# Clustered attention followed by an MLP: heads in pairs in a hand-given order, transposes from SBUF, argmax by block transposes, MLP pieces spread over the next batch

## The chip, the cores and the metric

The kernel runs on one core of a Trainium2 chip. The metric is the device time of one execution in microseconds (us). All runs named here were in the fast state but one, a run of e16 that is left out of its median. A profiled execution's span (582.5 us for the kernel before) is the time that the trace covers; it differs from the median time by under 2%. PE is the matrix engine (TensorE), PEld its weight loads; VectorE is DVE, ScalarE is ACT, GpSimd is POOL, and SyncE (SP) issues most transfers in these kernels. A suffix q (SPq, ACTq) marks an engine's queue of issued transfers and waits. In the timelines below each engine works through its own instructions in the order in which the program gives them. PSUM is the memory into which the matmuls write; a buffer there is free again once another engine has read it out.

## The reference, cut to what matters

```python
# q, k, v: (4 batches, 8 heads, 768 tokens, 64); centroids: (8 heads, 16, 64)
q_assign = argmax(q_n @ c_n.T);  k_assign = argmax(k_n @ c_n.T)      # normalised rows
mask   = q_assign[:, :, :, None] == k_assign[:, :, None, :]
scores = where(mask, q @ k.T / 8, -1e9)
attn   = exp(scores - max);  attn /= sum(attn)
x      = (attn @ v), heads side by side                              # (3072, 512)
h      = x @ w_in                                                    # (3072, 2048)
out    = (h * sigmoid(h)) @ w_out                                    # (3072, 512)
```

Both kernels write each token's cluster as a one-hot of 16 rows below the 64 rows of q and k, so that one matmul over 80 rows gives score and mask. The exp runs on the transposed scores. The row of ones beside v gives the denominators, and the attention output is multiplied by their reciprocals before the MLP (called MoE in the code). The clusters come from "logits": q and k are split into a high and a low f16 part (128 rows), multiplied by the centroids' high part and, for accuracy, by their low part.

## The kernel before

One head at a time goes through stages that a software pipeline spaces out. The order within an engine is chosen by the framework. The parts that matter:

```python
wout_s = ...; nc.gpsimd.dma_start(wout_s, moe_w_out...)       # 2 MB of f16 in one transfer, w_in likewise
nc.vector.tensor_scalar(out=wout_s, in0=wout_s, scalar1=0.5, ...)     # L59
... # stage_p2, p3: hl -> DRAM scratch, then dma_start_transpose(ab, DRAM)
def stage_l(bh):                                              # logits of one head, q and k
    for ti, ab in enumerate((qab, kab)):
        g = ti * 32
        for half in range(2):
            nc.tensor.matmul(dst, stk[:, h],   ab[:, sl],    start=True, stop=False)   # 128 rows
            nc.tensor.matmul(dst, clT32[:, h], ab[0:64, sl], start=False, stop=True)   # 64 rows
    nc.scalar.copy(Lsb[:, 0], psL...); nc.scalar.copy(Lsb[:, 1], psL...)
    nc.gpsimd.partition_all_reduce(mx, Lsb, channels=16, reduce_op=max)     # L176
# stage_l2: oh_sb = Lsb >= mx (VectorE); stage_m: one-hots into ab[64:80]
# stage_b1: scores and exp (L199); stage_b2: P @ v; stage_z1, z2: denominators out,
#           reciprocal, back as one row, partition_broadcast on GpSimd, multiply on VectorE
# MoE of a 384-token block: 16 pieces A (h, tanh, product), then 3 pieces B (output)
```

The softmax here doesn't subtract the row's maximum and nothing guards it: scores larger than these inputs give would overflow.

## Time and profile before

| | before |
|---|---|
| median time | 579.92 us (first three runs), 579.76 us (four) |
| first exp, last exp (start) | 72.3 us, 478.9 us |
| PE busy | 437.3 us, 75% of the span |
| mean granted clock | 0.899 |

The page's first part (busy time, share of the span, instructions):

```profile
PE 437.3 (75%) x1922; PEld 201.6 (35%) x1922; DVE 326.3 (56%) x498; ACT 301.2 (52%) x419; POOL 217.0 (37%) x104
```

The page's fourth part, the chain of waits that ended last, by engine:

```profile
PE 36%; ACT 15%; DVE 14%; POOL 14%; DMA 11%; issue 8%; SPq 2%; DVEq 0%; POOLq 0%; ACTq 0%
```

Busy time by stretch: start, attention, and what is left after the last exp. In each row come the stretch, its length, and busy us with the number of instructions for PE, PEld, DVE, ACT and POOL; then the granted clock, the DMA engines' busy share and GB/s.

```profile
0.00:72.00 72.00, 15.89 (x38) 3.96 (x39) 27.84 (x66) 8.87 (x11) 28.07 (x20) 1.00 0.95 174
72.00:480.00 408.00, 335.46 (x1468) 157.24 (x1468) 256.66 (x361) 259.32 (x353) 185.76 (x82) 0.86 0.44 89
480.00:583.00 103.00, 86.01 (x417) 40.37 (x415) 41.83 (x72) 33.05 (x57) 3.14 (x3) 0.99 0.09 32
```

The reader should see that no engine is full: PE is on the chain for 36% of the time only, and the clock in the middle is 0.86, so part of PE's "busy" time is matmuls at half speed (384-column matmuls stand 0.16 us apart in dense stretches and 0.32 us after a gap of 2.84 us, at 214 us).

Two details: the first is VectorE's wait at the start, a timeline line (start, duration, instruction, and in brackets the idle time before it and what ended it). The second is the pace of the logit matmuls: the timeline's first column shows them 0.27 us apart for 384 columns, taking turns between 128 and 64 rows.

```profile
27.46 2.29 DVE L59 TENSOR_SCALAR wout_s<-wout_s 128x8192 f16<-128x8192 f16 x1 [21.21 <-DMA wout_s<-in_moe_w_out_dram]
...
219.42 0.33 PE L171 MATMUL psL<-ab_1456,clT_89 64*32 64x384 f16 x1
219.68 0.34 PE L170 MATMUL psL<-ab_1456,stk 128*32 128x384 f16 x1
219.95 0.33 PE L171 MATMUL psL<-ab_1456,clT_89 64*32 64x384 f16 x1
```

### The profile page before, as it was taken

How to read it: one execution, taken by the hardware profiler on the slowest of the kernel's cores; microseconds unless marked ns; L12 is line 12 of the kernel's file. 1: busy time of each engine (PE TensorE's matmuls, PEld its weight loads, DVE VectorE, ACT ScalarE, POOL GpSimd, SP SyncE). 2: the span in 40 equal slices, each digit the busy share in tenths (PEclk: the TensorE clock that was granted, in tenths of full speed). 3: DMA queues.
4: the chain of work that ended last, by engine and by line, in shares of the span. 5: the costliest groups of instructions: out<-in, count | busy, mean ns of one | idle time of the engine just before them, and what ended most of it. 6: DMA issues, size and time to landing. Idle time of an engine off the chain costs nothing.

```text
span 582.5 us, 5887 instructions
## 1 busy us (share of the span) xinstructions
PE 437.3 (75%) x1922; PEld 201.6 (35%) x1922; DVE 326.3 (56%) x498; ACT 301.2 (52%) x419; POOL 217.0 (37%) x104
## 2 busy tenths in 40 slices
PE   0005489757688578998578798789898999897976
PEld 0001134323233233444234344334444454343433
DVE  2162699975848966687855535442455335425251
ACT  1002377648368575747476447664487393415150
POOL 1053854655466544444474235444433002000000
PEclk9999998769679678799798898779798999999999
DMA  8999566957455544857552212323120100100101
GB/s 155 190 150 245 125 182 156 152 116 117 76 110 117 87 119 102 161 137 222 98 108 35 36 54 37 48 33 60 46 30 1 41 17 20 38 37 19 52 2 55
DMA packets 106190, 52.20 MB, mean 90 GB/s; under 512 B 84080, under 2 KB 102512, under 8 KB 106160
## 3 DMA queue, kind: packets, MB, share of 16 engines
q1 hardware_dynamic: 78480, 44.49, 30.8%
q0 software_dynamic: 27680, 7.34, 13.2%
q8 instruction: 15, 0.25, 0.2%
q14 instruction: 15, 0.12, 0.1%
HBM read 27.49 MB, written 19.07 MB: 80 GB/s over the span
## 4 chain that ended last, share of the span: by engine, by line
PE 36%; ACT 15%; DVE 14%; POOL 14%; DMA 11%; issue 8%; SPq 2%; DVEq 0%; POOLq 0%; ACTq 0%
POOL mx L176 13%; PE po L265 10%; PE ph L254 9%; ACT P L199 6%; DMA wout_s<-in_moe_w_out_dram 4%; ACT tn L259 4%; DVE gt L260 4%; PE pO L209 4%; PE psL L170 4%; PE psL L171 3%; PE pST L196 3%; DVE oh_sb L182 3%; ACT Lsb L174 2%; PE pO L210 2%; DMA rzd<-rzt 1%
## 5 line engine op out<-in xcount | busy, mean ns | idle before, releaser
L199 ACT ACTIVATE P<-pST,bias_77 128x768 f16<-128x768 f32 x192 | 161.5, 909 | 65.3 <-PE pST L197 64.1
L176 POOL PARTITION_ALL_REDUCE mx<-Lsb x32 | 153.7, 4807 | 109.8 <-ACT Lsb L174 109.7
L259 ACT ACTIVATE tn<-ph,zbias 128x384 f32<-128x384 f32 x128 | 73.0, 588 | 105.1 <-PE ph L254 104.2
L260 DVE SCALAR_TENSOR_TENSOR gt<-tn,ph 128x384 f16<-128x384 f32 x128 | 68.7, 551 | 80.9 <-ACT tn L259 80.1
L182 DVE TENSOR_TENSOR oh_sb<-Lsb,mx 16x1536 f16<-16x1536 f32 x32 | 66.8, 2087 | 66.5 <-POOL mx L176 66.5
L265 PE MATMUL po<-wout_s,gt 128*128 128x512 f16 x384 | 87.2, 383 | 2.7 <-DVE gt L260 2.7
L254 PEld LDWEIGHTS <-win_s 128*128 128x128 f16 x512 | 51.9, 101 | 96.7 <-issue 69.2
L209 PE MATMUL pO<-P,vt 128*65 128x512 f16 x192 | 84.1, 457 | 0.5 <-ACT osb L212 0.5
L254 PE MATMUL ph<-xt_73,win_s 128*128 128x384 f16 x128 | 44.2, 346 | 48.2 <-DVE gt L260 35.6
L173 ACT COPY Lsb<-psL 16x768 f32<-16x768 f32 x32 | 25.2, 788 | 93.9 <-PE psL L171 86.3
L142 POOL DMA_DIRECT2D vt<-in_v_dram x32 | 27.9, 878 | 88.1 <-DVE vt L141 54.5
L210 PE MATMUL pO<-P,vt 128*65 128x256 f16 x192 | 59.8, 311 | 0.0
L233 POOL PARTITION_BROADCAST rzb<-rzrow x32 | 34.6, 1082 | 66.8 <-DMA rzrow<-rzd 66.6
L265 PEld LDWEIGHTS <-gt 128*128 128x128 f16 x384 | 37.8, 99 | 47.9 <-issue 5.6
L254 PE MATMUL ph<-xt_74,win_s 128*128 128x384 f16 x128 | 44.4, 348 | 5.6 <-DVE xt_74 L234 5.6
L254 PE MATMUL ph<-xt_76,win_s 128*128 128x384 f16 x128 | 43.8, 342 | 5.5 <-DVE xt_76 L234 5.5
L254 PE MATMUL ph<-xt_75,win_s 128*128 128x384 f16 x128 | 44.0, 346 | 1.1 <-DVE xt_75 L234 1.1
L270 DVE COPY ot<-po 128x512 f32<-128x512 f32 x24 | 16.4, 687 | 41.4 <-PE po L265 41.2
L209 PEld LDWEIGHTS <-vt 128*65 128x65 f16 x192 | 25.4, 132 | 38.1 <-issue 27.3
L170 PEld LDWEIGHTS <-stk 128*32 128x32 f16 x128 | 12.2, 95 | 67.1 <-issue 64.5
L210 PEld LDWEIGHTS <-vt 128*65 128x65 f16 x192 | 24.9, 130 | 8.5 <-issue 1.5
L212 ACT COPY osb<-pO 65x768 f32<-65x768 f32 x32 | 25.6, 801 | 0.2 <-PE pO L210 0.2
(493 smaller groups left out, 508.4 us busy)
## 6 DMA issues: line engine op xcount, KB each, us to landing
out_dram<-ot SPq DMA_DIRECT2D x24, 256.0 KB
vt<-in_v_dram POOLq DMA_DIRECT2D x32, 96.0 KB, 3.9
win_s<-in_moe_w_in_dram POOLq DMA_DIRECT2D x1, 2048.0 KB, 13.6
wout_s<-in_moe_w_out_dram POOLq DMA_DIRECT2D x1, 2048.0 KB, 25.3
zd<-osb SPq DMA_DIRECT2D x32, 3.0 KB
zt<-zd SPq DMA_DIRECT2D x32, 3.0 KB
rzd<-rzt SPq DMA_DIRECT2D x32, 3.0 KB
rzrow<-rzd SPq DMA_DIRECT2D x32, 3.0 KB
```

The costliest lines, as they stand in the source:

```text
L142: nc.gpsimd.dma_start(vt[:, :, 0:64], v[b, h].rearrange("(j p) d -> p j d", j=NJ))
L170: nc.tensor.matmul(dst, stk[:, h], ab[:, sl], start=True, stop=False)
L176: nc.gpsimd.partition_all_reduce(mx, Lsb, channels=HC, reduce_op=bass_isa.ReduceOp.max)
L182: nc.vector.tensor_tensor(out=oh_sb, in0=Lsb, in1=mx, op=ALU.is_ge)
L199: nc.scalar.activation(out=P, in_=pST[:, 0:768], func=AF.Exp, bias=bias32, scale=ESC)
L209: nc.tensor.matmul(pO[:, 0:512], vt[:, j, :], P[:, 0:512], start=(j == 0), stop=(j == NJ - 1))
L210: nc.tensor.matmul(pO[:, 512:768], vt[:, j, :], P[:, 512:768], start=(j == 0), stop=(j == NJ - 1))
L233: nc.gpsimd.partition_broadcast(rzb, rzrow, channels=64)
L254: nc.tensor.matmul(ph, win_s[:, r, ts(fb, 128)], xts[r][:, T0 : T0 + MOE_T], start=(r == 0), stop=(r == NR - 1),)
L259: nc.scalar.activation(out=tn, in_=ph, func=AF.Tanh, bias=zbias, scale=0.5)
L260: nc.vector.scalar_tensor_tensor(out=gt[:, fb, :], in0=tn, scalar=1.0, in1=ph, op0=ALU.add, op1=ALU.mult)
L265: nc.tensor.matmul(po, gt[:, fc, ts(tsub, 128)], wout_s[:, fc, :], start=(fc == 0), stop=(fc == NFB - 1),)
```

## The change

The intent is to keep PE fed throughout. Two heads (a pair) are routed together. The clusters are found with VectorE's 32x32 block transposes, instead of ScalarE copies and GpSimd's maximum. The scratch in DRAM goes: transposes read SBUF. Denominators come back as a broadcast transfer to 64 partitions. Weights come in eight pieces. The 0.5 moves to the output copy. Every instruction stands in an order written by hand: the program is cut into slots, each with one score tile (six to a head, twelve to a pair), and each batch's MoE is cut into 56 pieces, spread over the slots of the next batch. The core of the diff:

```diff
-    for i in range(nbh + OF_P0 - OF_Z2):        # stages of one head, order by the framework
-        if valid(i): stage_p0(i)
-        ...
+    ctx.enter_context(tc.manual_schedule())
+    def logits(p):                              # a pair: 2 heads x (q, k) = 4 column groups
+        for u, (lo, hi) in enumerate(((0, 512), (512, 768))):
+            for i, w in enumerate((wh, wl)):    # both 128 rows
+                for h in range(2):
+                    for t in range(2):
+                        g = 32 * (2 * h + t)
+                        nc.tensor.matmul(psL[g : g + 32, 0 : hi - lo], w[:, 2 * r + h], ab[:, h, lo:hi], ...)
+    # route_a: lt = block transpose of psL; route_b: max over 16, compare, transpose back;
+    # route_c: one-hots into abt[64:80]
+    def z_bcast(p):
+        for h in range(2):
+            nc.sync.dma_start(rzb[64 * h : 64 * h + 64, :], rzs[p][h : h + 1, :].to_broadcast([64, S]))
+    def z_mul(p, h):                            # the normalisation, VectorE
+        nc.vector.tensor_tensor(out=xts[r][o, ...], in0=osbs[2 * p + h][o, :], in1=rzbs[p][o, :], op=ALU.mult)
+    ...
+    for p in range(NP):
+        s0 = 12 * p
+        at(s0 + 0, logits(p + 1));   at(s0 + 1, route_a(p + 1));  at(s0 + 3, route_b(p + 1))
+        at(s0 + 4, route_c(p + 1, 0)); at(s0 + 5, route_c(p + 1, 1))
+        at(s0 + 6, split(p + 2, 0), turn(p + 2, 0))
+        at(s0 + 8, split(p + 2, 1), turn(p + 2, 1))
+        at(s0 + 9, load_v(p + 2));   at(s0 + 9, load_qk(p + 3))
+        at(s0 + 12, z_out(2 * p));   at(s0 + 18, z_out(2 * p + 1))
+        at(s0 + 20, z_recip(p));     at(s0 + 22, z_bcast(p))
+        at(s0 + 24, z_mul(p, 0));    at(s0 + 25, z_mul(p, 1))
```

(The `at` lines are shortened: lambdas and bounds are left out, as are the slot loop and the bodies of the other functions.)

## The prediction

> **What bounds the kernel now.** No engine is the limit; chained waits are. The page gives PE 75% of 582.5 us, VectorE 56%, ScalarE 52%, GpSimd 37%. The chain of waits holds PE for only 36% and GpSimd's max across partitions (mx) for 13%. Three losses:
>
> 1. Start. In the timeline VectorE sits 21.2 us (6.3 to 27.5 us) behind the 2 MB w_out transfer, because the scaling by 0.5 stands first in its order. The first exp runs at 72 us.
> 2. Attention from 72 to 480 us is paced by the routing loop: psL -> two copies (0.79 us each) -> mx (4.67 us) -> oh_sb (1.75 us, up to 4.3 us while GpSimd works) -> scaled one-hots. PE idles meanwhile, and the granted clock is 0.80 from 72 to 200 us and 0.88 from 200 to 360 us (busy time by stretch). The dips are to 0.5 and follow gaps of some us. The Trainium skill, "TensorE: Matmul & The Clock Gate", Part 1, states an idle PE falls to half clock; the trace agrees (384-column matmuls 0.16 us apart, 0.32 after the 2.84 us gap at 214 us).
> 3. Tail. After 480 us there is nearly only MoE, and its first half is latency-bound: 2.07 us per two pieces, where the matmuls alone need 1.3. About 100 us.
>
> **What the change removes, adds, moves.** PE columns stay about the same: 786k, 328 us at the 0.42 ns per column that dense stretches show (48 matmuls of 512 in 10.5 us). Logit matmuls now stand 0.265 us apart for 384 columns (0.16 ideal), switching between 128 and 64 rows each time. After, four column groups alternate in one shape: I expect 2.5 us per pair instead of 4.2 (estimate).
>
> GpSimd loses mx (154 us) and the broadcast (35 us). ScalarE loses 50 us of psL copies. VectorE, per pair (estimate from its 0.36/0.55/0.95 us instructions): split 3.2, three block transposes 1.9, max and compare 1.0, one-hots 1.4, normalise 1.9: 9.5 us, so 240 us in all against 326. DMA loses 12.6 MB of scratch writes and gains 6 MB of broadcast. The SBUF transposes are the unknown: SyncE took 1.2 us to issue each DRAM one; these are twice as large, I guess 3 to 5 us each.
>
> **Sum (estimates).**
> - Start to first exp: 34 us (the identity still waits for GpSimd, at 15.3 us before; then split, transposes, cold logits, routing).
> - 62 slots without MoE, 1.1 us each (ScalarE needs 0.92, PE 0.85): 68.
> - 130 slots with MoE. PE per slot: 1536 attention + 2048 MoE columns = 1.49, logits 0.21, gaps 0.05: 1.75, so 228. Plus 1.5 us for each of 12 pairs where psL and MoE compete for three PSUM buffers: 18.
> - Last 14 slots and the wait for the last normalisation: 19.
> - Last batch's MoE alone: 98k columns, 41 us dense, plus fill and store: 47.
> - In-order stalls (SyncE, weights competing with loads): 11.
>
> Total **425 us**, 8 in 10 between 395 and 470. Chance of faster by over 2%: 0.97; same 0.02; slower 0.01.
>
> **What would show it.** First exp near 34 us; PE above 85% busy with clock near 1.0 from about 100 to 350 us; no PE wait behind w_out or mx; exps about 1.1 us apart early and 1.75 later; last exp near 350 us; tail about 47 us with first-half pieces 0.7 us apart. Busy: GpSimd under 80 us, ScalarE near 250, VectorE near 240.
>
> **What would make it wrong.** SBUF transposes issued or moved so slowly that SyncE (in order, with stores and denominators behind them) paces each pair; VectorE blocked in order on the denominator broadcast, two slots after its issue; the psL/MoE buffer contest larger than 1.5 us. In the other direction, column groups running truly together, or fewer stalls, give 390 us.

## The result, and the profile after

The changed kernel takes 471.12 us (median of four runs, 468.27 to 473.52) against 579.76 us; the ratio is 0.811 (95% interval 0.806 to 0.816). It is correct. Ratios here are formed from fast runs of the same rounds, so not quite the ratio of the medians quoted. The direction was right. The time lies just outside the range (395 to 470), and 46 us above the 425 forecast.

The page's first part, the chain's shares by engine, and the first item by line:

```profile
PE 358.7 (76%) x1922; PEld 179.2 (38%) x1922; DVE 240.3 (51%) x432; ACT 259.5 (55%) x387; POOL 23.6 (5%) x52
...
PE 38%; DMA 23%; DVE 20%; SPq 10%; ACT 4%; issue 4%; DVEq 0%; ACTq 0%
DMA rzb<-rzd 16%; PE ph L230 13%; PE po L244 12%; PE pv L184 6%; SPq L115 4%; DMA abt<-hl 4%; PE st L167 4%; DVE hl L110 3%; DVE gt L235 3%; DMA zt<-osb 3%; SPq L92 2%; SPq L99 2%; DVE abt L156 2%; PE st L168 2%; DVE hl L109 2%
```

The engines' work fell as it was meant to (GpSimd 24 us, ScalarE 260, VectorE 240), but PE is still only 76% busy. The largest item of the chain is a transfer: rzb, the broadcast of the reciprocal denominators. Busy time by stretch, cut at the first exp, at the 62nd (where the MoE of the first batch begins) and at the last:

```profile
0.00:21.00 21.00, 5.45 (x37) 1.93 (x38) 15.86 (x44) 2.86 (x3) 3.80 (x14) 1.00 0.82 206
21.00:124.00 103.00, 61.73 (x313) 28.06 (x311) 43.37 (x73) 58.30 (x79) 11.13 (x20) 0.84 0.69 152
124.00:404.00 280.00, 231.54 (x1278) 119.31 (x1277) 151.25 (x266) 175.74 (x267) 8.64 (x18) 0.91 0.36 91
404.00:472.00 68.00, 59.96 (x300) 29.89 (x298) 29.83 (x50) 22.57 (x40) 0.00 (x0) 0.93 0.13 47
```

| stage | predicted us | measured us |
|---|---|---|
| start to first exp | 34 | 21 |
| 62 slots without MoE | 68 | 103 |
| 130 slots with MoE (228 + 18) | 246 | 280 |
| last 14 slots, wait, last MoE (19 + 47) | 66 | 68 |
| in-order stalls, not placed | 11 | in the rows above |

The two middle rows hold the error: +35 and +34 us. The list of waits (engine, line and waiter, what it waited for: total us, times, longest us) names the suspects. The first line is PE waiting for the pairs' transposes. The other four are one instruction, the normalisation, for four output tiles, 87.3 us together. (A tenth of this wait is missing from the four lines: 10.7 us more at xt_71 are put down to a copy on ScalarE, but that wait ends at 86.11 us, 0.09 us after the broadcast's landing, as in the neighbouring pairs. With it VectorE stands for 98 us.)

```profile
PE psL L127 <- DMA abt<-hl: 43.6, 19, 6.5
DVE xt_73 L216 <- DMA rzb<-rzd: 33.2, 4, 10.9
DVE xt_72 L216 <- DMA rzb<-rzd: 24.4, 4, 10.1
DVE xt_70 L216 <- DMA rzb<-rzd: 18.9, 4, 9.3
...
DVE xt_71 L216 <- DMA rzb<-rzd: 10.8, 2, 5.6
```

One pair in the MoE stage shows how it comes about. First SyncE's timeline, then VectorE's and PE's:

```profile
304.96 1.45 SPq L115 DMA_TRANSPOSE abt<-hl  x1
306.51 0.82 SPq L249 DMA_DIRECT2D out_dram<-ot  x1
307.42 0.40 SPq L99 DMA_DIRECT2D natv<-in_v_dram  x1
307.88 0.50 SPq L92 DMA_DIRECT2D nat_2632<-in_q_dram  x1
308.43 0.54 SPq L92 DMA_DIRECT2D nat_2634<-in_k_dram  x1
309.07 1.14 SPq L210 DMA_DIRECT2D rzb<-rzd  x2
...
308.26 0.55 DVE L235 SCALAR_TENSOR_TENSOR gt<-tn,ph 128x384 f16<-128x384 f32 x1 [0.74 <-ACT tn L234]
315.92 0.95 DVE L216 TENSOR_TENSOR xt_72<-osb,rzb 64x768 f16<-64x768 f32 x1 [7.11 <-DMA rzb<-rzd]
...
317.39 0.48 PE L230 MATMUL ph<-xt_70,win_s 128*128 128x384 f16 x1 [6.12 <-DVE gt L235]
```

SyncE issues 1.2 MB of loads of q, k and v (three transfers of 384 KB) and then the broadcast. VectorE reaches the normalisation at 308.8 us, before the broadcast has even been issued (309.07 us), and stands for 7.11 us. Behind it, in its order, stand the MoE products and the emptying of the logits, so the three PSUM buffers that MoE and logits share stay full, and PE stands for 6.12 us. After that gap matmuls run at half clock (384 columns 0.32 us apart, from 317.66 to 317.98 us; before it, at 310.12 us, they stood 0.16 us apart). "TensorE: Matmul & The Clock Gate", Part 1, of the Trainium skill says that an idle PE falls to half clock; this trace agrees. The page's sixth part gives the broadcast's time from issue to landing, a median of 5.7 us:

```profile
rzb<-rzd SPq DMA_DIRECT2D x32, 192.0 KB, 5.7
```

The landing is only part of the wait. The broadcast stands two slots ahead of its use in the program, but that lead is one of order and not of time: in 9 of the 16 pairs VectorE came to the normalisation before SyncE had issued the broadcast, and in the four pairs without MoE 3.5 to 4.6 us before. One of those, from the timelines of SyncE and VectorE (VectorE came at 75.46 us):

```profile
79.98 1.12 SPq L210 DMA_DIRECT2D rzb<-rzd  x2
86.11 1.94 DVE L216 TENSOR_TENSOR xt_71<-osb,rzb 64x768 f16<-64x768 f32 x2 [10.65 <-ACT osb L190]
```

### The profile page after: what moved, and what is told of

It is laid out like the page before. It is cut to its first block, busy times and chain, and to the rows that moved or that the text cites. A ratio compares the mean times of both kernels' runs of the same rounds, so it can differ in the third digit from the quotient of the medians.

```text
span 471.7 us, 5345 instructions
## 1 busy us (share of the span) xinstructions
PE 358.7 (76%) x1922; PEld 179.2 (38%) x1922; DVE 240.3 (51%) x432; ACT 259.5 (55%) x387; POOL 23.6 (5%) x52
## 4 chain that ended last, share of the span: by engine, by line
PE 38%; DMA 23%; DVE 20%; SPq 10%; ACT 4%; issue 4%; DVEq 0%; ACTq 0%
DMA rzb<-rzd 16%; PE ph L230 13%; PE po L244 12%; PE pv L184 6%; SPq L115 4%; DMA abt<-hl 4%; PE st L167 4%; DVE hl L110 3%; DVE gt L235 3%; DMA zt<-osb 3%; SPq L92 2%; SPq L99 2%; DVE abt L156 2%; PE st L168 2%; DVE hl L109 2%
## 5 line engine op out<-in xcount | busy, mean ns | idle before, releaser
L170 ACT ACTIVATE P<-st,bias_74 128x768 f16<-128x768 f32 x192 | 171.5, 903 | 99.6 <-PE st L168 98.7
L167 PE MATMUL st<-abt 80*128 80x512 f16 x192 | 80.9, 422 | 1.3 <-ACT P L170 0.5
L168 PE MATMUL st<-abt 80*128 80x256 f16 x192 | 56.4, 294 | 0.0
L127 PE MATMUL psL<-abt,wh 128*32 128x512 f16 (+1 forms) x128 | 21.2, 409 | 45.1 <-DMA abt<-hl 43.6
L190 ACT COPY osb<-pv 128x384 f32<-128x384 f32 x64 | 30.6, 478 | 15.6 <-PE pv L184 15.4
L167 PEld LDWEIGHTS <-abt 80*128 80x128 f16 x192 | 20.3, 106 | 19.8 <-issue 9.6
L168 PEld LDWEIGHTS <-abt 80*128 80x128 f16 x192 | 20.3, 106 | 17.9 <-issue 9.0
L247 DVE TENSOR_SCALAR ot<-po 128x512 f32<-128x512 f32 x24 | 16.4, 684 | 18.4 <-PE po L244 18.2
L216 DVE TENSOR_TENSOR xt_73<-osb,rzb 64x768 f16<-64x768 f32 x8 | 7.6, 953 | 33.3 <-DMA rzb<-rzd 33.2
L156 DVE TENSOR_SCALAR abt<-oh 16x768 f16<-16x768 f16 x64 | 23.3, 364 | 1.6
L184 PE MATMUL pv<-P,vb_80 128*128 128x384 f16 x72 | 19.7, 359 | 1.6 <-ACT osb L190 1.6
L216 DVE TENSOR_TENSOR xt_72<-osb,rzb 64x768 f16<-64x768 f32 x8 | 7.6, 952 | 24.5 <-DMA rzb<-rzd 24.4
```

The lines of the kernel that those rows point to most:

```text
L127: nc.tensor.matmul(psL[g : g + 32, 0 : hi - lo], w[:, 2 * r + h], ab[:, h, lo:hi], start=(i == 0), stop=(i == 1),)
L156: nc.vector.tensor_scalar(out=ab[64 : 64 + HC, h, :], in0=ohs[p][g : g + HC, :], scalar1=OHV, scalar2=None, op0=ALU.mult)
L167: nc.tensor.matmul(st[:, 0:512], kt[0:K, ts(j, 128)], qt[0:K, 0:512], start=True, stop=True)
L168: nc.tensor.matmul(st[:, 512:768], kt[0:K, ts(j, 128)], qt[0:K, 512:768], start=True, stop=True)
L170: nc.scalar.activation(out=P, in_=st[:, 0:768], func=AF.Exp, bias=bias32, scale=ESC)
L184: nc.tensor.matmul(po[:, 0:CH], vt[:, j, :], Ps[i, j][:, ts(u, CH)], start=(j == 0), stop=(j == NJ - 1))
```

## The experiments

Theory W: VectorE's in-order wait for the broadcast paces the pairs, and the broadcast is late because of the loads in front of it. Rival T: the SBUF transposes, the risk that the prediction priced as SyncE's issue time, pace the pairs; PE's 43.6 us of waits for them are the evidence for it. Times are medians of four runs (five for e18, the three fast ones for e16). Ratios to the kernel before, with 95% intervals, stand where a verdict needs them.

**e1: a constant in place of the denominators** (all transfers stay). Its output is wrong, which doesn't matter for the time.

```diff
-            out=xts[r][o, ...], in0=osbs[2 * p + h][o, :], in1=rzbs[p][o, :], op=ALU.mult
+            out=xts[r][o, ...], in0=osbs[2 * p + h][o, :], in1=rz_c[o, 0:1].to_broadcast([64, S]), op=ALU.mult
```

> The normalisation multiplies by a constant tile instead of the broadcast denominators (wrong result on purpose); every transfer stays. Theory W (VectorE, in order, waits 87 us for the broadcast; behind it stand routing and split, so the loop normalise, route, split, turn, loads, broadcast paces a pair at 20 us): VectorE's 87 us of waits at the normalisation go, pairs of the first batch take 14 us instead of 20, total 400 to 425 us. Rival T (the transposes, issued late and landing late, pace the pairs: PE waits 44 us for them): at most 15 us gained, total 455 to 470, PE still waits 35 us or more for the transposes.

390.83 us (ratio 0.675): 80 us less, more than expected. The multiplication itself takes as long as before (0.95 us), so the gain is the wait's. PE's waits for transposes fall too, from 43.6 us to the line below, without any edit to them, so about a third of them was an effect of the other wait:

```profile
PE psL L129 <- DMA abt<-hl: 28.3, 12, 6.7
```

The stages are now 87, 219 and 61 us. Theory W holds: of the 98 us of waiting, 80 were on the path.

**e2: the normalisation 4 slots later.**

```diff
-        at(s0 + 24, z_mul(p, 0));  at(s0 + 25, z_mul(p, 1))
+        at(s0 + 28, z_mul(p, 0));  at(s0 + 29, z_mul(p, 1))     # last pair unmoved; MoE of a batch starts 4 slots later
```

> The normalisation is moved from slots 24 and 25 to 28 and 29 of its pair (last pair unmoved), so the broadcast has 6 slots to land. Theory W: nearly as good as the constant denominator, 405 to 435 us, VectorE waits at the normalisation under 20 us. Rival T: 455 to 475 us.

415.92 us (0.718). VectorE waits at the normalisation for 9.7 us, although the broadcast lands no sooner (5.9 us). As theory W said.

**e3: loads behind the broadcast.**

```diff
-        at(s0 + 9, load_v(p + 2));   at(s0 + 9, load_qk(p + 3))
+        at(s0 + 11, load_v(p + 2));  at(s0 + 11, load_qk(p + 3))
```

> The loads of q, k, v (1.2 MB a pair) move from slot 9 to slot 11, behind the broadcast in SyncE's order instead of ahead of it. Theory W1 (the broadcast lands after 5.7 us because it stands behind 1.2 MB of loads on the same queue): landing falls to 2.5 to 3.5 us, total 425 to 450 us. Rival W2 (the broadcast of one DRAM row to 64 partitions is slow in itself): landing stays over 5 us, total 462 to 475.

413.37 us (0.714, interval 0.709 to 0.718): 58 us for a change of one number, better than expected. The broadcast's landing in the page's sixth part, a little above the 2.5 to 3.5 us expected:

```profile
rzb<-rzd SPq DMA_DIRECT2D x32, 192.0 KB, 3.7
```

So the broadcast is not slow in itself; the loads ahead of it make it late. VectorE still waits 47.8 us at the normalisation. The stages after the first exp, cut at the 62nd and the last one's start:

```profile
20.80:116.50 95.70, 62.53 (x314) 28.63 (x313) 45.46 (x74) 58.56 (x80) 10.51 (x18) 0.84 0.74 160
116.50:343.80 227.30, 211.28 (x1277) 112.57 (x1276) 150.09 (x266) 174.39 (x268) 10.62 (x20) 1.00 0.45 114
343.80:410.00 66.20, 58.34 (x298) 29.18 (x296) 29.86 (x50) 22.29 (x40) 0.00 (x0) 0.97 0.14 48
```

The MoE stage fell from 280 to 227 us, which is 1.75 us for each of its 130 slots; the prediction had said 1.75 (see below for how far that is luck). PE does the same work in 211 us busy instead of 232, at a clock of 1.00 instead of 0.91. This is how about 3.5 us a pair (2.0 us of landing and about 1.4 us of SyncE's time for issuing the three loads) may have become nearly 5 us a pair: the gaps had also slowed the matmuls after them. (That last link is an argument from the clock column, not a separate run.)

**e4: split and transposes at slots 2 and 4 instead of 6 and 8.**

```diff
-        at(s0 + 6, split(p + 2, 0), turn(p + 2, 0));  at(s0 + 8, split(p + 2, 1), turn(p + 2, 1))
+        at(s0 + 2, split(p + 2, 0), turn(p + 2, 0));  at(s0 + 4, split(p + 2, 1), turn(p + 2, 1))
```

> Split and transposes of a pair move from slots 6 and 8 to slots 2 and 4, 8 to 10 slots ahead of the logits that need them. Rival T: PE's 44 us of waits for the transposes fall under 10 us and the total to 430 us or less. Theory W: those waits fall too, but the broadcast still paces: 445 to 472 us, VectorE still waits 60 us or more at the normalisation.

464.19 us (0.802), 7 us better. VectorE still waits 71.0 us for the broadcast, and PE still 43.5 us for the transposes, which both theories had expected to fall: a slot number is only a place in the order, and the splits still stand behind the waiting normalisation. So this edit did not remove the waits for transposes and can't tell what they cost. Rival T falls as the main cause by e1 to e3, which gain 55 to 80 us while 28.3 to 37.3 us of waits for transposes remain. What those cost was tested by no run.

**e5: e2 and e3 together.**

> Normalisation 4 slots later and loads behind the broadcast, together. If both remove the same wait (theory W), their gains of 55 and 58 us don't add: 393 to 408 us, close to the 391 of the constant denominator, VectorE waits under 10 us at the normalisation. If they remove different waits, the gains add: below 380 us.

414.46 us (0.713). VectorE waits 5.4 us at the normalisation. The gains don't add, so e2 and e3 remove the same wait; but the time stays above e1's 391 and over 6 us above the expected band. A delay of the normalisation seems to have a price of its own (see e15).

**e6: loads issued by GpSimd, at slot 9 as in the changed kernel.**

```diff
-            nc.sync.dma_start(nat, ...)      # natv likewise
+            nc.gpsimd.dma_start(nat, ...)
```

> As the changed kernel (loads at slot 9, normalisation at 24), but the loads of q, k, v are issued by GpSimd, which has its own queue. If the broadcast is late because it stands behind the loads in one queue's order: landing falls to 3 to 4 us, total 405 to 425 us. If the loads keep the shared DMA engines busy, whatever the queue: landing stays over 5 us, total 455 to 475 us.

434.27 us (0.747), between the two bands, landing 3.7 us. The timeline says: GpSimd, in order too, waits for PE before its copies of v (195.7 us of waits in the two copies), and its loads went out about 7 us ahead of the broadcast and, but for the first pair, had landed. The run tells nothing about the queue; e16 and e17 replace it.

**e7: e3, normalisation at slots 30 and 31, transposes at 3 and 5.**

> Loads at slot 11, normalisation at slots 30 and 31, split and transposes at slots 3 and 5. With VectorE no longer waiting for the broadcast, the earlier transposes can land before the logits: PE waits for transposes under 12 us (37 in the runs with one edit), total 375 to 392 us. If the transposes were not a limit of their own, 393 to 408 us as with two edits.

435.43 us (0.748), 22 us worse than e3 and above both bands. VectorE now waits at the split for its own loads, a wait that the other versions don't have:

```profile
DVE hl L109 <- DMA nat<-in_q_dram: 25.5, 8, 6.2
```

The loads had moved two slots later and the split three earlier.

**e8: the kernel before with one edit,** the scaling of w_out by 0.5 moved from VectorE's start to the output copy.

> The kernel before with one edit: w_out is not scaled by 0.5 on VectorE at the start, the output copy scales instead. Theory: VectorE's 21 us wait for w_out at the start goes, first exp 15 to 22 us earlier (from 72 us), total 555 to 568 us. Rival: the 4 MB of weights on the same DMA engines delay the first loads and transposes as much: total 572 to 580 us.

569.88 us (0.981, interval 0.977 to 0.985; a small gain clear of noise, though "unclear" by the record's threshold of 2%). The exps begin 9 us earlier, at 63.4 us. Both bands were missed: the gain of about 11 us lies between them. It is some 10% of the 109 us that the whole change won.

**e9, e10, e11: onward from e3.** e9 issues the eight weight pieces every 8th slot from slot 8 on. e10 also paces the third batch's MoE to last until slot 212, so that PE has work while the last denominators travel. e11 also moves split and transposes to slots 5 and 7.

```diff
-        if s < 2 * HB * 6 and s % 2 == 1 and wloads:          # e9
+        if s >= 8 and s % 8 == 0 and wloads:
-    NSL = LAST + 14                                            # e10, with the end of the last queue set to NSL
+    NSL = LAST + 20
```

> Loads behind the broadcast, and the eight weight pieces issued every 8th slot from slot 8 on instead of every 2nd from slot 1. Theory: the first two pairs take 21 to 24 us each because 8 MB of weights share the DMA engines (busy 0.93 there) with transposes and loads; spread out, these pairs take 13 to 17 us like the third and fourth, total 395 to 405 us. Rival (the first pairs are slow from cold start and routing): no change, 408 to 418 us.

> As the run before, and the third batch's MoE pieces are paced to last until slot 212 instead of 206, so PE has work while the last denominators go out and come back. Theory: PE's idle gap of about 10 us before the last batch's MoE shrinks by half, total 5 to 8 us less than the run before. Rival: no gain, the wait only moves.

> As the run before, and split and transposes one slot earlier (5 and 7). If the transposes still pace the pairs without MoE (PE waits 2 to 3 us for them at each pair): 3 to 8 us less. If the split then waits for its loads: no gain or a loss.

e9: 405.47 us (0.698), a little above the expected band. Twelve-slot steps between exps in the timeline show that the first two pairs take 12.6 and 15.5 us instead of 24.1 and 20.9, but the step from slot 48 to slot 61 grew from 17.8 to 22.3 us: the last weight pieces now fall there (that they are the cause was not tested). e10: 400.60 us (0.690, interval 0.687 to 0.693), 5 us less. The expected gap of 10 us before the last MoE was in fact 3.3 us in e9; in e10 there is none. e11: 411.79 us (0.709), a loss; the split did not wait for its loads, but the waits for the denominators' transfer at the reciprocal grew from 15.4 to 28.1 us.

**e12: logits with the high and the low part of one column group next to each other** (on e3).

```diff
-            for i, w in enumerate((wh, wl)):
-                for h in range(2):
-                    for t in range(2):
+            for h in range(2):
+                for t in range(2):
+                    for i, w in enumerate((wh, wl)):
```

> Loads behind the broadcast (413 us), and the logit matmuls in the order in which the high and the low part of one column group follow each other, instead of four groups in turn. The changed kernel does a pair's 16 logit matmuls in 1.4 us even at half clock, which one after the other would need 5 us: four groups run side by side. Theory: in the grouped order they run one after another or in pairs, 2 to 4 us a pair, 16 pairs, most of it on PE's path: 428 to 455 us. Rival (order is indifferent): 410 to 418 us.

414.79 us (0.713; e3 had 0.714). The order is indifferent. **e13** is e10 in this order, and with the low part over 64 rows, as the kernel before has it:

```diff
-                            psL[g : g + 32, 0 : hi - lo], w[:, 2 * r + h], ab[:, h, lo:hi],
+                            psL[g : g + 32, 0 : hi - lo], w[0:K, 2 * r + h], ab[0:K, h, lo:hi],     # K = 128, 64
```

> The version with loads, weights and tail mended (400.6 us), logits grouped by column group, and the low part with 64 rows as in the kernel before, so 128 and 64 rows alternate. Theory (the change of rows drains the array and keeps the groups apart): a pair's logits take 3.5 to 5 us instead of 0.8, total 425 to 455 us. Rival (groups overlap whatever the rows): 398 to 406 us.

436.10 us (0.752): 35.5 us more than e10. PE's timeline in e10 is in the first fence (lines of four matmuls merged), in e13 in the second:

```profile
189.87 0.40 PE L127 MATMUL psL<-abt,wh 128*32 128x512 f16 x4
190.09 0.39 PE L127 MATMUL psL<-abt,wl 128*32 128x512 f16 x4
190.31 0.28 PE L127 MATMUL psL<-abt,wh 128*32 128x256 f16 x4
190.42 0.28 PE L127 MATMUL psL<-abt,wl 128*32 128x256 f16 x4
190.63 0.39 PE L167 MATMUL st<-abt 80*128 80x512 f16 x1
```

```profile
211.38 0.39 PE L128 MATMUL psL<-abt,wh 128*32 128x512 f16 x1
211.70 0.39 PE L128 MATMUL psL<-abt,wl 64*32 64x512 f16 x1
...
215.62 0.39 PE L168 MATMUL st<-abt 80*128 80x512 f16 x1
```

With one shape, four matmuls of 512 columns on four column groups take 0.22 us together, and a pair's 16 take 0.76 us; with rows changing, they go one by one, 0.32 us apart, 4.24 us a pair. (Sixteen pairs at this rate would lose 56 us; part is hidden, as PE's waits for transposes fall from 29.5 to 15.4 us.) "TensorEngine Tiling (Array Packing)", Key Properties, of the Trainium skill says that changing the tiling mode drains TensorE, and that tiles of one mode work in parallel; both agree with these runs.

**e14: e10 with the constant, and e15: e10 with the normalisation at slots 27 and 28.**

> The version at 400.6 us with a constant tile in place of the broadcast denominators (wrong result on purpose). If the 48 us of waits at the normalisation are by now off the path: 394 to 401 us. If they still cost: 375 to 388 us.

> The version at 400.6 us with the normalisation at slots 27 and 28. If the waits still cost: 385 to 395 us. If they are off the path, or the later start of each batch's MoE takes the gain back: 398 to 408 us.

e14: 388.68 us (0.669), 12 us less than e10, between the two bands. Counted exp by exp, most of the gain lies in the MoE stage: the 62nd exp starts at 103.4 us instead of 106.8, and the stage from there to the last exp, in e10 (first line) and in e14, is 10 us shorter:

```profile
106.80:332.10 225.30, 207.79 (x1253) 110.69 (x1252) 146.54 (x260) 172.53 (x262) 12.40 (x21) 1.00 0.46 114
103.40:318.60 215.20, 206.48 (x1253) 110.19 (x1251) 145.45 (x258) 171.48 (x262) 10.28 (x21) 1.00 0.46 121
```

e15: 400.80 us (0.690), no gain, although VectorE's waits at the normalisation are down from 48.3 to 3.7 us. That doesn't clear the normalisation, since e14 changes nothing else and gains. The exps point to the second branch of the expectation: the four pairs in which a batch's MoE begins, now three slots later, take 93.7 us together instead of 88.8, and the rest of that stage 4.2 us less (in e5 these four take 92.1 us, in e3 87.2). No run tests this alone. **e18** is e15 with the reciprocal one slot later, behind the second split in VectorE's order:

```diff
-        at(s0 + 20, z_recip(p))
+        at(s0 + 21, z_recip(p))          # last pair unmoved
```

> As the run with the normalisation 3 slots later (400.8 us), and the reciprocal one slot later, so behind the second split in VectorE's order instead of ahead of it. If the reciprocal's wait for its transfer (15 us in all) paces the pairs without MoE: 388 to 396 us. If not: 398 to 404 us.

396.53 us (0.681, interval 0.678 to 0.684; e15 0.690, 0.686 to 0.695). Just above the band of 388 to 396, but clear of e15, and the waits at the reciprocal are down from 18.2 to 6.8 us. The edit takes away the same kind of fault a second time, an instruction that waits for a small transfer ahead of the split that the next pair needs. But the trace doesn't put the gain where it was expected: from the first to the 62nd exp e18 takes 86.4 us and e15 85.5, and in the MoE stage 223.3 and 226.0. The two profiled executions are only 1.4 us apart, so where the gain comes from stays open. This is the best correct version: 0.681/0.811 = 0.84 of the changed kernel's time.

**e16 and e17: queue or engines?** e16 issues the loads from ScalarE, e17 only the broadcast; slots as in the changed kernel.

```diff
-            nc.sync.dma_start(nat, ...)                        # e16, natv likewise
+            nc.scalar.dma_start(nat, ...)
-            nc.sync.dma_start(rzb[64 * h : ...], ...)          # e17
+            nc.scalar.dma_start(rzb[64 * h : ...], ...)
```

> The changed kernel with the loads of q, k, v at slot 9 issued by ScalarE instead of SyncE, the broadcast at slot 10 still by SyncE. If one queue's order makes the broadcast late: landing 3 to 4.2 us with loads in flight, total 405 to 430 us. If the engines are shared whatever the queue: landing 5 us or more, total 450 to 475 us.

> The changed kernel with only the broadcast issued by ScalarE, loads at slot 9 by SyncE as before. If one queue's order makes it late: landing 3 to 4.2 us, total 405 to 430 us. If the engines are shared whatever the queue: landing 5 us or more, total 450 to 475 us.

454.37 us (0.789; a fourth run, 461.08 us, was slow) and 431.02 us (0.742). The first lies in the band of shared engines, the second 1 us above that of queue order. e16's time says little about the broadcast, as its first exp comes at 27.8 us instead of 21.0 and PE waits 64.9 us for transposes. The landing is 4.7 us (median; 3.2 to 8.4) in both, between the two expected bands (up to 4.2, and 5 or more) and between the 5.7 and 3.7 us of the changed kernel and e3:

```profile
rzb<-rzd ACTq DMA_DIRECT2D x32, 192.0 KB, 4.7
```

A queue of its own takes away only part of the delay; loads in flight slow the broadcast on another queue too. The Trainium skill, "DMA: Bandwidth & Descriptors", Rules for kernel authors, states that transfers from all issuing engines run on the same 16 DMA engines and interleave; the 4.7 us agree with that. How the 2 us divide between queue order and shared engines stays open, because the issue times differ between the runs: the last load goes out 1.2 to 11 us ahead of the broadcast in e16; in e17 the loads go out from 0.7 us ahead of it to 2.5 us behind it. What is shown are two cures: issue the small urgent transfer first (e3), or leave it time (e2).

## Why the prediction was right or wrong

**Right: the direction and the engines' work.** GpSimd's maximum, ScalarE's copies and the waits behind w_out go. How much of the 109 us each of these brought was not tested, but for the 11 us of e8. GpSimd, ScalarE and VectorE busy times were forecast as under 80, near 250 and near 240 us, and measured as 23.6, 259.5 and 240.3. The tail was forecast as 66 us and measured as 68.

**Wrong: the step "in-order stalls (SyncE, weights competing with loads): 11".** The prediction built its sum from engine work per slot and added a small remainder for order. It even listed "VectorE blocked in order on the denominator broadcast, two slots after its issue" among the risks, and did not price it. "Two slots after its issue" is a lead of 2 to 3.5 us only if both engines keep step. The runs showed that they did not: VectorE came to the normalisation before the broadcast's issue in 9 of 16 pairs, the broadcast then took 5.7 us to land behind 1.2 MB of loads, and 98 us of waiting came of it. Removing the wait is worth 80 us (e1), moving the loads behind the broadcast 58 us (e3), leaving the broadcast four slots more 55 us (e2). The stage that was off by 34 us is the one that e3 brings to 1.75 us a slot, against the 1.75 (plus 1.5 us a pair) forecast: the order term failed. That the work term looks exact is partly luck. It held 0.21 us a slot for logits, which measure 0.76/12 = 0.06; the difference is about what PE still stands idle in e3 (227.3 − 211.3 = 16 us, or 0.12 a slot).

**Wrong: 1.1 us a slot without MoE.** It took 103/61 = 1.69 us. With the weights spread and the denominators' two waits mended (e18) it is still (107.6 − 21.1)/61 = 1.42 us. Two causes were found: the broadcast (the stage falls from 103 to 96 us in e3, and to 87 in e1), and the weights beside the first two pairs' transposes (from 96 to 87 in e9). The rest, about 18 us over the forecast, stays open. It is not the wait at the normalisation, since even e14 takes 83 us. PE's waits for transposes, 15.2 us in this stage of e18, are the suspect, and no run tests them.

**Wrong, the other way: logits at 2.5 us a pair.** They take 0.76 us at full clock. The prediction named two things, four groups taking turns and one shape: the turns don't matter (e12), the shape does (e13).

**Wrong, the other way: 34 us to the first exp.** It comes at 21 us. The prediction took the identity's late end (15.3 us before) as a fixed delay. In the changed kernel no weight transfer stands ahead of it on GpSimd, and it starts at 1.0 us. (No run tests this alone.)

**Wrong: the price of issuing the transposes.** Issuing an SBUF transpose of twice the size takes SyncE 1.45 us (median), not 3 to 5, except beside the weights (up to 7.6 us). The contest for PSUM buffers, priced at 18 us in all, was not measured alone; in e3 the whole MoE stage fits the estimate without it, with the luck told above.

## What to carry to other kernels

In a hand-given order, price each wait as a transfer's landing time plus what delays its issue, and don't count slots between issue and use as time: the slots order each engine by itself, and here VectorE came to the use before SyncE came to the issue. Then ask what stands behind the waiting instruction on that engine. Issue small urgent transfers ahead of bulk loads, since a queue of their own helped here only in part (4.7 us against 3.7). When a wait seems to be the cause, replace its data by a constant first: that run tells what a cure of this wait could win, and here it showed at once that 80 us were to be had. And count events one by one before placing a gain in a stage: the first exp of a pair without MoE can stand 8 to 10 us after the one before it, so being off by one or two there moves a gain of that size to another stage.

## What the Trainium skill lacked or had wrong

- "TensorEngine Tiling (Array Packing)" names the drain on a change of tiling mode but gives no cost: with 128x32 and 64x32 matmuls alternating, 512-column matmuls stood 0.32 us apart where those of one shape stand 0.22 us apart even one by one, a pair's 16 logit matmuls took 4.24 us instead of 0.76, and the kernel 436.10 us instead of 400.60.
- "TensorE: Matmul & The Clock Gate", Part 3, gives 2.38 times for three column tiles of 512 columns, and no figure for four. Here four column groups of 32 gave four 512-column matmuls every 0.22 us, the time in which the dense MoE stretches do one (48 in 10.5 us). The page's figure is for the span of one pack and ours for the spacing in a stream, so the two need not clash. Its note on the XBUSes in Part 2 calls quadrant 3 not supported and doesn't say what that rules out; all runs with the fourth group at partitions 96 to 127 and real denominators were correct.
- "DMA: Bandwidth & Descriptors" says, of bandwidth, that issuing from several engines only saves issue time; it gives no figure for how late a small transfer lands beside bulk loads. Measured for a broadcast in two transfers of 192 KB: 5.7 us behind 1.2 MB of loads on the same queue, 4.7 us from another queue beside them, 3.7 us issued ahead of them (medians; issue times differ between the runs, so the 4.7 is no clean measure of the queue).
- On none of the pages did I find what a GpSimd-issued transfer costs the GpSimd instruction behind it. Here the identity's last instruction started at 15.27 us behind two 2 MB weight transfers, and at 1.01 us without them. The profile names no releaser for the 11.74 us of idle time before it, so that the transfers held it is inferred.
